# A mixer-and-MLP kernel: first weight matrix in three loads, and another order of loads, products and engines

## The chip, the core and the metric

The kernel runs on one core of one Trainium2 chip. The metric is device time in microseconds (us) of one execution. Five executions of the kernel before took 136.20, 135.62, 136.43, 135.65 and 136.16 us: median 136.16. One further view, the profile, is of one execution that took 136.2 us, of which the program's own instructions span 134.9; the remaining 1.3 us lie around them.

The core has five engines that run side by side and meet at semaphores. TensorE (PE) multiplies matrices; its weight loads are shown as PEld. VectorE (DVE), ScalarE (ACT) and GpSimd (POOL) work elementwise. SyncE (SP) only issues transfers (DMAs). DMAs of one issuing queue are served in the order of their issue.

## What is computed

`x` has 2048 rows (tokens) of 512 bfloat16 numbers. The weights are `w1` and `w2` (512 x 512), `w3` (512 x 1792) and `w4` (1792 x 512).

```python
def reference(x, w1, w2, w3, w4):
    B, S, D = x.shape
    h = _gelu(_layernorm(x, axis=-1) @ w1)
    c = D // 4
    g0 = jnp.pad(h[:, :, 0*c:1*c], ((0, 0), (1, 0), (0, 0)))[:, :S, :]
    ...
    g3 = jnp.pad(h[:, :, 3*c:   ], ((0, 0), (0, 2), (0, 0)))[:, 2:, :]
    hs = jnp.concatenate([g0, g1, g2, g3], axis=-1) @ w2
    x1 = x + hs
    h2 = _gelu(_layernorm(x1, axis=-1) @ w3) @ w4
    return x1 + h2
```

The four quarters of `h` are shifted by 1, -1, 2 and -2 tokens before they meet `w2`. So the second product of a tile of tokens needs `h` of that tile and of both its neighbours.

## The kernel before, in words

**Tiles.** The tokens are cut into 16 tiles of 128, called t0 to t15. A tile passes these steps; q is the tile's number in the first layer and 16 plus the number in the second.

1. Load `dma_x` (line 366), and statistics by `ln` (line 380). For q in `STAT_ACT` ScalarE makes the sums (lines 389 and 394) and DVE two small instructions; for the others DVE does it with `bn_stats` and `bn_aggr` (lines 410 and 412). POOL raises the variance to -1/2 (line 417).
2. Normalization on the engine that `NORM` names: DVE (line 438, the default), ACT (line 447) or POOL (line 450). For the last two, DVE or POOL (`NMR`) first makes one more small number (line 443). Tile 0 is special (`NAT`, `SPLIT`): its mean alone is subtracted, in two halves of 256 columns (line 428), and the scale is applied later, in the gelu (line 562).
3. Transposition. q = 0 to 5, 16 and 17 are transposed on PE with an identity matrix (steps `sa`, `sb` and `ty`, line 483), and copied out of PSUM by DVE or ACT (line 491, choice `EVAC`). The other 24 are transposed by a DMA, `tp`q (line 456), issued by SP after the normalization.
4. `up1`: the product with `w1` (line 619; for tile 0 steps `ra` and `rb`, line 521, each over two of the four K chunks of 128), gelu on ACT (line 634). Tile 0's result is turned by step `th` (line 587).
5. `mix`: the product with the shifted `h` and `w2` (line 659), and the residual on DVE (lines 666 and 670).
6. The same normalization and transposition for the second layer, then `up2` (line 619, 56 matmuls for one group) and gelu.
7. `down` (line 688, 14 matmuls a tile), residual on DVE (line 696), and the store (line 699). The last tile's product is done in pieces of 256, 128 and 128 columns.

`GROUPS` says how many tiles `up1` and `up2` take at once: a group of one streams 128 columns a matmul, of two 256, of four 512.

**What sets the order.** `SCRIPT` is the order of PE's work, written out; PE follows it strictly. It begins with `warm`, products of zeros that need no data. `LOADS` is the order of the input loads, all on SP's queue but `x0`, which ACT issues. An entry `tp`n in `LOADS` stands for that DMA transpose where there is one: tp9 for example is tied between its neighbours, while `tp16` names a tile that PE turns and has no effect. The order on the other engines comes from a planner (`Program.order` and `Program.place`), which runs when the program is built. It walks through a model of the engines with a cost for each operation (`dur`), and at each step gives an engine the ready operation with the smallest due time; due times are counted back from PE's script, starting at `DUE`. Loads get numbers far below all due times (line 736), so SP issues a load whenever one is free to go, and DMA transposes after that. An entry tied ahead of a load inherits a number below that load's (lines 141 to 143). `RESTART` adds time in the model to a load that follows something else than a load on its queue. What the planner leaves is a fixed order for each engine.

`emit` (line 766) writes that order with semaphore waits. A weight load is complete only when all its pieces are; `up2` waits for all four K chunks of `w3`, `down` for all fourteen of `w4`.

Of the kernel before, what the change touches and what calls it, by code (L numbers as in the profile page):

```python
# [25 lines left out]
class Program:  # L26
# [2 lines left out]

    HOP = {"pe": 200.0, "dve": 155.0, "act": 220.0, "pool": 120.0, "sp": 70.0}  # L30
    LOOK = {"dve": 300.0, "act": 300.0}
    DUE = 385824.0
    BEGIN = {"sp": 30.0, "act": 150.0, "pe": 400.0, "dve": 150.0, "pool": 450.0}
    ENTRY = 1900.0
    COLD, RESTART = 4300.0, 800.0
# [16 lines left out]
    def order(self):  # L52
# [58 lines left out]
        assert seen == len(self.ops), "cycle"  # L111
        if self.DUE:

            topo, left = [], [len(d) for d in preds]
            stack = [i for i, n in enumerate(left) if n == 0]
            while stack:
                i = stack.pop()
                topo.append(i)
                for j in succs[i]:
                    left[j] -= 1  # L120
                    if left[j] == 0:
                        stack.append(j)
            due, t = {}, self.DUE
            for op in self.ops:
# [12 lines left out]
        for op in self.ops:  # L137
            op.prio += BIAS.get(op.name, 0.0)
            if op.first is not None:
# [11 lines left out]
    def place(self, succs, order_only):  # L151
# [8 lines left out]
        rings = {"sp": [], "act": []}  # L160
        fed = {}
        clock = moved = last = self.total = 0.0
# [35 lines left out]
        def land(op):  # L198
            nonlocal moved, last
            if op.queue == "tp":  # L200
                at = max(clock + 500.0, op.start + 2450.0, last + 600.0) + self.LAG["tp"]
            elif op.name.startswith("out"):
                at = clock + 300.0
                self.total = max(self.total, at)
            else:
                moved += op.dur
                at = clock + 600.0 + min(600.0, 0.3 * moved) + (600.0 if op.dur > 1400.0 else 0.0) + self.LAG["load"]
            if op.queue != "tp":
                last = max(last, at)
            op.landed = at  # L210
            for j in succs[op.idx]:
                if (op.idx, j) not in order_only:
                    release(op, self.ops[j], at + 30.0)

        while len(out) < len(self.ops):
            while True:
                best = None
                for e in ENGINES:
                    if cands[e]:
                        t = max(free[e], min(ready[o.idx] for o in cands[e]))  # L220
                        if best is None or t < best[0]:
# [12 lines left out]
            if op.queue:  # L234
                tp = op.queue == "tp"
                free[e] = start + (1300.0 if tp else 500.0)
                load = op.name.startswith("dma")
                work = 600.0 if tp else op.dur + (self.RESTART if load and not fed.get(e, True) else 0.0)
                fed[e] = load
                rings[e].append([start + (1400.0 if tp else 1000.0), work, op])  # L240
                for j in succs[op.idx]:
                    if (op.idx, j) in order_only:
                        release(op, self.ops[j], None)
            else:
                dur = op.dur
# [9 lines left out]
        self.seq = out  # L255
        return out

GROUPS = {1: (1, 1, 1, 1, 2, 1, 4, 2, 1, 2), 2: (2, 4, 4, 4, 2)}
NORM = {4: "act", 6: "pool", 8: "pool", 9: "pool", 10: "pool", 12: "act", 14: "pool", 15: "pool", 19: "pool", 20: "pool", 22: "act", 23: "act", 24: "act", 25: "act", 27: "pool", 28: "act", 31: "act"}
EVAC = {1: "both", 2: "dve", 3: "both", 4: "both", 5: "dve", 6: "dve", 8: "both", 11: "dve", 16: "both", 17: "dve", 18: "dve", 20: "dve", 21: "both", 22: "dve", 29: "dve", 30: "dve", 31: "dve"}  # L260
STAT_ACT = (0, 4, 8, 11, 15, 17, 18, 19, 20, 21, 25, 26, 27, 28, 29, 30, 31)
TAIL = (256, 128, 128)
NMR = {1: "pool", 3: "pool", 5: "pool", 10: "pool", 11: "pool", 12: "pool", 13: "pool", 15: "pool", 17: "pool", 20: "pool", 21: "pool", 25: "pool", 26: "pool", 27: "pool", 28: "pool", 30: "pool", 31: "pool"}
NAT = (0,)
SPLIT = (0,)
CSPLIT = ()
HEV = {0: "dve", 2: "dve"}
BIAS = {}
LOADS = """
x1 x2 tp16 w1a w1b x4 x3 w2 x5 x6-7 x9-10 x0@act tp17 x11 w3a w3b x8 w4b w4a tp9 x12-13 x14-15  # L270
"""
SCRIPT = """
warm:10 sa:0 sb:0 ty:1 ra:0 rb:0 ty:2 up1:1 th:0 up1:2 mix:0 ty:3 mix:1 ty:4-5 up1:3-4 mix:2 ty:16-17 mix:3
up2:0 mix:4 up1:5 down:0-1 mix:5 up1:6-7 mix:7-8 up1:9 mix:9-10 up1:8 mix:6 mix:15 up2:1 mix:11-12 up2:2
mix:14 down:4 down:2 down:6 mix:13 up2:4 down:3 down:8 down:5 up2:3 down:7 down:12 down:11 down:10 down:9
down:14 down:13 down:15
"""

def bass_standalone__mixer_s_mlp__prompt_kernel(nc, x, w1, w2, w3, w4, out):
# [14 lines left out]
    with ExitStack() as es:  # L294
        sb = lambda name, shape, dt: es.enter_context(nc.sbuf_tensor(name, shape, dt))
# [22 lines left out]
        warm = sb("warm", [P, 1], F32)  # L318
# [41 lines left out]
        def load(item):  # L360
            name, _, eng = item.partition("@")
            eng = eng or "sp"
            if name[0] == "x":
                a, _, b = name[1:].partition("-")
                t0, t1 = int(a), int(b or a) + 1
                yield pg.add(eng, f"dma_x{t0}", lambda e: e.dma_start(x_sb[:, t0:t1, :], xt[:, t0:t1, :]),
                             writes=[(("x", t), 0) for t in range(t0, t1)], dur=(t1 - t0) * 380.0, queue=eng)
            else:
                dst, src = {"w1": (w1_sb, w1), "w2": (w2_sb, w2), "w3": (w3_sb, w3), "w4": (w4_sb, w4)}[name[:2]]
                n = src.shape[0] // P  # L370
                c0, c1 = {"": (0, n), "a": (0, n // 2), "b": (n // 2, n)}[name[2:]]
                op = pg.add(eng, f"dma_{name}",
                             lambda e: e.dma_start(dst[:, c0:c1, :],
                                                   src.rearrange("(c p) f -> p c f", p=P)[:, c0:c1, :]),
                             writes=[((name[:2], c), 0) for c in range(c0, c1)],
                             dur=(c1 - c0) * P * src.shape[1] * 2 / (345.0 if src.shape[1] == D else 400.0), queue=eng)
                yield op


        def ln(layer, t):  # L380
# [3 lines left out]
            col = lambda a: a[:, q : q + 1]  # L384
            if q in STAT_ACT:
                if layer == 1:
# [22 lines left out]
            else:  # L409
# [4 lines left out]
                       writes=[(("mv", q), 0), (("vpe", q), 0)], dur=75)  # L414
            var = vpe[:, q : q + 1] if q in STAT_ACT else mv[:, q, 1:2]
            pg.add("pool", f"rstd{q}",
                   lambda e: e.tensor_tensor(col(rstd), var, neghalf[:], ALU.pow),  # L417
                   reads=[(("vpe", q), 0), (("neghalf",), 0)], writes=[(("rstd", q), 0)], dur=470)
            how = NORM.get(q, "dve")
            dst = xn_buf[:, slot(q), :]  # L420
# [19 lines left out]
            else:  # L440
                eng = NMR.get(q, "dve")
                pg.add(eng, f"nmr{q}",
# [200 lines left out]
        def mm_mix(t):  # L643
# [220 lines left out]
```

## Time and profile before

| | |
|---|---|
| median of five runs | 136.16 us |
| the profiled execution | 136.2 us |
| its span | 134.9 us |
| PE busy | 131.4 us (97%) |
| ACT, DVE, POOL busy | 61.0, 50.2, 27.5 us |
| read from HBM, written | 6.82 MB, 2.10 MB |
| DMA transposes | 24, median 2.5 us from issue to landing |
| matmuls recorded | 777 |

Times in the profile are us from the span's start, unless marked ns. The page cuts the span into 40 slices of 3.37 us, with a digit for the busy tenths of each engine. A matmul's recorded length includes its passage through the array, so the time that one costs is read from where the next one starts: in the chain of work, sixteen of 128 columns take 0.89 us (0.056 each), 56 of 256 take 6.11 (0.109 each) and eight of 512 take 1.73 (0.216 each). A few matmul records are missing; the chain then shows 0.05 us of "issue" that is no idle time.

### The profile page before, as it was taken

What the parts mean: (1) busy time and instruction counts of PE and PEld (TensorE: products, weight loads), DVE (VectorE), ACT (ScalarE), POOL (GpSimd) and SP (SyncE); (2) the same over time, 40 slices, a digit from 0 to 9 for tenths busy, and PEclk for the clock granted to TensorE, in tenths of its full rate; (3) what the DMA queues carried; (4) which work ended last, traced back from release to release, by engine and by line L of the source; (5) the groups of instructions that cost most, each with busy time, mean ns of one, the idle gap of its engine ahead of it and who ended that gap; (6) DMA issues with size and microseconds to landing.
All of it is one profiled execution on the core that took longest, in us unless ns stands there. A gap on an engine that the chain in (4) does not pass through costs nothing.

```text
span 134.9 us, 2033 instructions
## 1 busy us (share of the span) xinstructions
PE 131.4 (97%) x777; PEld 72.0 (53%) x790; DVE 50.2 (37%) x156; ACT 61.0 (45%) x100; POOL 27.5 (20%) x61
## 2 busy tenths in 40 slices
PE   8999999999999999999999999999999999999994
PEld 3477688544665444444444448844444444444463
DVE  3679988876177810060004226013200002232222
ACT  6678877662527997577554005510055530000000
POOL 2431569499204321006001001000000000000000
PEclk9999999999999999999999999999999999999999
DMA  5899999954551253000300311101110001111112
GB/s 159 266 345 415 363 335 85 222 119 88 110 119 36 45 115 78 0 0 0 78 0 5 78 39 39 39 0 44 39 39 0 0 0 39 39 42 41 39 41 78
DMA packets 21338, 12.20 MB, mean 90 GB/s; under 512 B 13904, under 2 KB 20816, under 8 KB 21328
## 3 DMA queue, kind: packets, MB, share of 16 engines
q1 hardware_dynamic: 20752, 11.80, 34.6%
q10 hardware_dynamic: 576, 0.26, 0.7%
q8 instruction: 6, 0.10, 0.3%
q14 instruction: 4, 0.03, 0.1%
HBM read 6.82 MB, written 2.10 MB: 66 GB/s over the span
## 4 chain that ended last, share of the span: by engine, by line
PE 97%; issue 1%; DVE 0%; POOLq 0%
PE y_ps L619 46%; PE o_ps L688 36%; PE o_ps L659 10%; PE o_ps L712 3%; PE y_ps L483 2%; PE y_ps L521 1%; DVE o_sb L696 0%; PE o_ps L587 0%; POOLq L849 0%
## 5 line engine op out<-in xcount | busy, mean ns | idle before, releaser
L619 PE MATMUL y_ps<-xnT,w_sb 128*128 128x512 bf16 (+2 forms) x420 | 63.4, 308 | 0.2
L619 PEld LDWEIGHTS y_ps<-xnT,w_sb 128*128 128x128 bf16 x424 | 38.3, 98 | 24.9 <-ACT h2T L634 0.3
L688 PE MATMUL o_ps<-w_sb,h2T 128*128 128x512 bf16 (+2 forms) x249 | 48.7, 355 | 0.2
L634 ACT ACTIVATE h2T<-y_ps 128x1024 bf16<-128x1024 f32 (+1 forms) x29 | 28.6, 993 | 24.1 <-PE y_ps L619 23.8
L688 PEld LDWEIGHTS o_ps<-w_sb,h2T 128*128 128x128 bf16 x252 | 23.5, 98 | 24.7
L696 DVE TENSOR_TENSOR o_sb<-o_ps,x_sb 128x512 bf16<-128x512 f32 (+2 forms) x18 | 11.4, 633 | 47.5 <-PE o_ps L688 47.5
L394 ACT ACTIVATE junk<-x_sb 128x512 bf16<-128x512 bf16 x17 | 10.6, 621 | 14.5 <-DVE x_sb L666 14.4
L417 POOL TENSOR_TENSOR rstd<-vpe,neghalf 128x1 f32<-128x1 f32 x17 | 9.4, 559 | 34.5 <-DVE vpe L406 34.5
L666 DVE SCALAR_TENSOR_TENSOR x_sb<-o_ps,x_sb 128x512 bf16<-128x512 f32 x12 | 8.2, 682 | 19.9 <-PE o_ps L659 19.8
L659 PE MATMUL o_ps<-w_sb,hT 128*128 128x512 bf16 x58 | 14.8, 379 | 0.5 <-DVE xn_buf L438 0.3
L417 POOL TENSOR_TENSOR rstd<-mv,neghalf 128x1 f32<-128x1 f32 x15 | 8.2, 548 | 19.5 <-DVE mv L412 18.6
L410 DVE BATCH_NORM_STATS2 st<-x_sb 128x6 f32<-128x512 bf16 x15 | 10.1, 681 | 3.2 <-DMA x_sb<-in_x_dram 3.0
L634 ACT ACTIVATE hT<-y_ps 128x512 bf16<-128x512 f32 (+1 forms) x10 | 8.1, 807 | 6.3 <-PE y_ps L619 6.3
L659 PEld LDWEIGHTS o_ps<-w_sb,hT 128*128 128x128 bf16 x64 | 6.1, 98 | 6.0 <-DVE xn_buf L438 0.2
L438 DVE TENSOR_SCALAR xn_buf<-x_sb,mv,rstd 128x512 bf16<-128x512 bf16 x14 | 6.2, 443 | 4.4 <-POOL rstd L417 4.3
L450 POOL TENSOR_SCALAR xn_buf<-x_sb,rstd,nmr 128x512 bf16<-128x512 bf16 x9 | 7.2, 801 | 1.3 <-DVE nmr L443 0.9
L447 ACT ACTIVATE xn_buf<-x_sb,nmr,rstd 128x512 bf16<-128x512 bf16 x8 | 6.3, 806 | 0.9 <-DVE nmr L443 0.6
L712 PE MATMUL o_ps<-zeros 128*128 128x512 bf16 x10 | 4.4, 632 | 0.6 <-POOLq L849 0.6
L406 DVE SCALAR_TENSOR_TENSOR vpe<-sums,mv 128x1 f32<-128x1 f32 x17 | 2.9, 173 | 3.2 <-ACT junk L394 2.8
L670 DVE TENSOR_TENSOR x_sb<-o_ps,x_sb 128x512 bf16<-128x512 f32 x4 | 2.7, 681 | 3.2 <-PE o_ps L659 3.2
L483 PEld LDWEIGHTS y_ps<-ident,xn_buf 128*128 128x128 bf16 x32 | 2.5, 111 | 1.9 <-issue 0.6
L389 ACT ACTIVATE junk<-x_sb 128x512 bf16<-128x512 bf16 x5 | 3.1, 628 | 1.0 <-DMA x_sb<-in_x_dram 0.8
(34 smaller groups left out, 32.9 us busy)
## 6 DMA issues: line engine op xcount, KB each, us to landing
w_sb<-in_w_dram SPq DMA_DIRECT2D x4, 896.0 KB, 10.9
out_dram<-o_sb SPq DMA_DIRECT2D x15, 128.0 KB, 1.7
x_sb<-in_x_dram SPq DMA_DIRECT2D x4, 256.0 KB, 5.0
x_sb<-in_x_dram SPq DMA_DIRECT2D x7, 128.0 KB, 4.5
w_sb<-in_w_dram SPq DMA_DIRECT2D x2, 256.0 KB, 4.2
w_sb<-in_w_dram SPq DMA_DIRECT2D x1, 512.0 KB, 6.2
xnT<-xn_buf SPq DMA_TRANSPOSE x24, 2.5
x_sb<-in_x_dram ACTq DMA_DIRECT2D x1, 128.0 KB, 2.5
```

The costliest lines, as they stand in the source:

```text
L394: (lambda d: (lambda e: e.activation(d, src, ACT_F.Square, accum_out=sums[:, q, 1:2])))(junk[:, b, :]),
L410: pg.add("dve", f"bnst{q}", lambda e: e.bn_stats(st9[:, q, 0:6], src), reads=rs, writes=[(("st", q), 0)], dur=605)
L417: lambda e: e.tensor_tensor(col(rstd), var, neghalf[:], ALU.pow),
L447: f = lambda e: e.activation(dst, src, ACT_F.Identity, bias=nmr[:, q : q + 1], scale=rstd[:, q : q + 1])
L450: f = lambda e: e.tensor_scalar(dst, src, rstd[:, q : q + 1], nmr[:, q : q + 1], ALU.mult, ALU.add)
L619: ins = e.matmul(y_ps[:, p, W * i : W * (i + 1)], wsb[:, dc, P * fc : P * (fc + 1)], src[:, dc, P * t0 : P * t0 + W], start=(dc == 0), sto ...
L634: (lambda d, s: (lambda e: e.activation(d, s, ACT_F.Gelu_apprx_tanh)))(dst, ysrc),
L659: ins = e.matmul(dst, hT[:, j, c0 : c0 + P], w2_sb[:, j, :], start=(j == 0), stop=(j == DC - 1))
L666: f = lambda e: e.scalar_tensor_tensor(x1_sb[:, t, :], dst, 1.0, x_sb[:, t, :], ALU.mult, ALU.add, accum_out=sums[:, NT + t, 0:1])
L688: ins = e.matmul(dst, h2T[:, fc, P * t : P * (t + 1)], w4_sb[:, fc, cs], start=(fc == 0), stop=(fc == FC - 1))
L696: (lambda d, c: (lambda e: e.tensor_tensor(o_sb[:, oi, c], d, x1_sb[:, t, c], ALU.add)))(dst, cs),
L712: ins = e.matmul(o_ps[:, b, :], zeros[:, 0:P], zeros[:], start=True, stop=True)
```

## The change

`w1` came in two halves (chunks 0-1 and 2-3). Now it comes as a half (`w1a`) and two quarters (`w1r`, `w1s`), with `x0` between them in the list. `w2` and `w3` are cut in the same way, and `w4` into four pieces (3, 4, 3 and 4 of its 14 chunks). `x4-5`, `x13-14` share a load, others come alone.

PE's script has eleven warm-up products instead of ten. The transposes of tile 1 stand between the two halves of tile 0's. t4 and t5 are groups of their own in `up1` where they had been a pair; t6-7 is now a pair, t8-9 a pair, t10-13 four. `mix:4` moves ahead of `up2:0`. In the second layer the groups become (2, 2, 4, 4, 4). The choices of engines are new throughout; the lists are in the diff. The planner charges `RESTART` only where its queue has run dry.

```diff
-    DUE = 385824.0
+    DUE = 316421.0
...
-                work = 600.0 if tp else op.dur + (self.RESTART if load and not fed.get(e, True) else 0.0)
+                dry = load and not fed.get(e, True) and clock + sum(h[1] for h in rings[e]) < start + 800.0
+                work = 600.0 if tp else op.dur + (self.RESTART if dry else 0.0)
...
-GROUPS = {1: (1, 1, 1, 1, 2, 1, 4, 2, 1, 2), 2: (2, 4, 4, 4, 2)}
-NORM = {4: "act", 6: "pool", 8: "pool", 9: "pool", 10: "pool", 12: "act", 14: "pool", 15: "pool", 19: "pool", 20: "pool", 22: "act", 23: "act", 24: "act", 25: "act", 27: "pool", 28: "act", 31: "act"}
-EVAC = {1: "both", 2: "dve", 3: "both", 4: "both", 5: "dve", 6: "dve", 8: "both", 11: "dve", 16: "both", 17: "dve", 18: "dve", 20: "dve", 21: "both", 22: "dve", 29: "dve", 30: "dve", 31: "dve"}
-STAT_ACT = (0, 4, 8, 11, 15, 17, 18, 19, 20, 21, 25, 26, 27, 28, 29, 30, 31)
+GROUPS = {1: (1, 1, 1, 1, 1, 1, 2, 2, 4, 2), 2: (2, 2, 4, 4, 4)}
+NORM = {0: "pool", 8: "act", 10: "act", 12: "pool", 13: "pool", 14: "pool", 15: "pool", 19: "act", 20: "act", 21: "pool", 22: "pool", 25: "act", 26: "act", 29: "act", 30: "act", 31: "pool"}
+EVAC = {0: "dve", 1: "both", 2: "both", 3: "both", 4: "both", 5: "both", 7: "both", 8: "dve", 9: "both", 10: "both", 11: "dve", 12: "dve", 13: "both", 14: "dve", 16: "both", 17: "dve", 18: "dve", 20: "dve", 22: "dve", 23: "dve", 26: "dve", 27: "both", 29: "dve", 30: "both"}
+STAT_ACT = (0, 6, 11, 14, 19, 20, 23, 25, 27, 31)
 TAIL = (256, 128, 128)
...
-HEV = {0: "dve", 2: "dve"}
-BIAS = {}
+HEV = {0: "dve", 4: "dve", 5: "dve"}
+BIAS = {"vpe0": -962.172}
 LOADS = """
-x1 x2 tp16 w1a w1b x4 x3 w2 x5 x6-7 x9-10 x0@act tp17 x11 w3a w3b x8 w4b w4a tp9 x12-13 x14-15
+tp4 x1 x2 w1a tp5 w1r x0@act w1s x3 x4-5 w2a w2r w2s tp3 tp2 tp4 w3a w3r tp5 w4q x9 tp1 x8 x7 x10 x6 w3s x11
+tp1 w4p w4s tp3 x12 w4r tp9 x13-14 x15
 """
 SCRIPT = """
-warm:10 sa:0 sb:0 ty:1 ra:0 rb:0 ty:2 up1:1 th:0 up1:2 mix:0 ty:3 mix:1 ty:4-5 up1:3-4 mix:2 ty:16-17 mix:3
-up2:0 mix:4 up1:5 down:0-1 mix:5 up1:6-7 mix:7-8 up1:9 mix:9-10 up1:8 mix:6 mix:15 up2:1 mix:11-12 up2:2
-mix:14 down:4 down:2 down:6 mix:13 up2:4 down:3 down:8 down:5 up2:3 down:7 down:12 down:11 down:10 down:9
-down:14 down:13 down:15
+warm:11 sa:0 ty:1 sb:0 ra:0 rb:0 ty:2 up1:1 th:0 up1:2 ty:3 mix:0-1 ty:4 up1:3 ty:5 up1:4 mix:2 up1:5 mix:3
+ty:16-17 mix:4 up2:0 up1:6 down:0-1 mix:6 up1:7 mix:5 up1:8 mix:8 mix:7 up2:1 mix:10 mix:9 up1:9 mix:11-12
+up2:2 mix:13 mix:15 up2:3 mix:14 down:5 down:2 down:6 down:3-4 down:7-8 up2:4 down:9 down:12 down:10 down:13
+down:11 down:14-15
 """
...
-                c0, c1 = {"": (0, n), "a": (0, n // 2), "b": (n // 2, n)}[name[2:]]
+                cut = lambda k: k * n // 4
+                a, b = {"": (0, 4), "a": (0, 2), "b": (2, 4), "p": (0, 1), "q": (1, 2), "r": (2, 3), "s": (3, 4)}[name[2:]]
+                c0, c1 = cut(a), cut(b)
```

More of the change, by code (lines that the diff above doesn't have):

```diff
@@ L256, in place @@
         return out
-GROUPS = {1: (1, 1, 1, 1, 2, 1, 4, 2, 1, 2), 2: (2, 4, 4, 4, 2)}
-NORM = {4: "act", 6: "pool", 8: "pool", 9: "pool", 10: "pool", 12: "act", 14: "pool", 15: "pool", 19: "pool", 20: "pool", 22: "act", 23: "act", 24: "act", 25: "act", 27: "pool", 28: "act", 31: "act"}
-EVAC = {1: "both", 2: "dve", 3: "both", 4: "both", 5: "dve", 6: "dve", 8: "both", 11: "dve", 16: "both", 17: "dve", 18: "dve", 20: "dve", 21: "both", 22: "dve", 29: "dve", 30: "dve", 31: "dve"}
-STAT_ACT = (0, 4, 8, 11, 15, 17, 18, 19, 20, 21, 25, 26, 27, 28, 29, 30, 31)
+GROUPS = {1: (1, 1, 1, 1, 1, 1, 2, 2, 4, 2), 2: (2, 2, 4, 4, 4)}
+NORM = {0: "pool", 8: "act", 10: "act", 12: "pool", 13: "pool", 14: "pool", 15: "pool", 19: "act", 20: "act", 21: "pool", 22: "pool", 25: "act", 26: "act", 29: "act", 30: "act", 31: "pool"}
+EVAC = {0: "dve", 1: "both", 2: "both", 3: "both", 4: "both", 5: "both", 7: "both", 8: "dve", 9: "both", 10: "both", 11: "dve", 12: "dve", 13: "both", 14: "dve", 16: "both", 17: "dve", 18: "dve", 20: "dve", 22: "dve", 23: "dve", 26: "dve", 27: "both", 29: "dve", 30: "both"}
+STAT_ACT = (0, 6, 11, 14, 19, 20, 23, 25, 27, 31)
 TAIL = (256, 128, 128)
-NMR = {1: "pool", 3: "pool", 5: "pool", 10: "pool", 11: "pool", 12: "pool", 13: "pool", 15: "pool", 17: "pool", 20: "pool", 21: "pool", 25: "pool", 26: "pool", 27: "pool", 28: "pool", 30: "pool", 31: "pool"}
+NMR = {1: "pool", 2: "pool", 3: "pool", 4: "pool", 5: "pool", 6: "pool", 8: "pool", 12: "pool", 14: "pool", 17: "pool", 18: "pool", 19: "pool", 21: "pool", 26: "pool", 27: "pool", 28: "pool", 29: "pool", 31: "pool"}
 NAT = (0,)
```

## The prediction

> **What bounds the kernel now.** I read the busy shares and slices first, then the chain of work that ended last in order of time, then the transfers one by one with their issue and landing, then the sums by stage.
>
> ```profile
> PE 131.4 (97%) x777; PEld 72.0 (53%) x790; DVE 50.2 (37%) x156; ACT 61.0 (45%) x100; POOL 27.5 (20%) x61
> ...
> PE   8999999999999999999999999999999999999994
> ...
> DVE  3679988876177810060004226013200002232222
> ...
> DMA  5899999954551253000300311101110001111112
> ```
>
> PE is busy 97% of the span, and from the second slice on it has almost nothing to win by being fed better. DVE and the transfers are full only in the first seven slices, some 23 us. So a gain or a loss is made there.
>
> ```profile
> 0.64 4.45 PE o_ps L712 x10
> 5.09 0.85 PE y_ps L483 x8
> 5.94 1.01 PE y_ps L521 x4
> ...
> 9.19 0.27 issue
> 9.46 0.81 PE o_ps L659 x3
> ...
> 11.35 0.31 PE y_ps L483 x4
> 11.66 0.02 issue
> 11.68 0.40 PE y_ps L483 x4
> ...
> 15.58 0.54 PE y_ps L483 x8
> 16.12 0.86 PE o_ps L659 x4
> 16.98 6.11 PE y_ps L619 x56
> 23.10 0.05 issue
> ```
>
> Columns: start, length, what. Three things are to be seen. The ten warm-up products end at 5.09; they start 0.427 us apart, and the eight transposes behind them take 0.106 each where later ones take 0.055, so PE's clock is still the slow one. Between 9.02 and 9.46 PE waits for `w2` (it landed at 9.15: issued at 2.98, 6.18 to landing; the chain puts the wait at 0.27, and one matmul record is missing, so 0.22 is lost). The transposes at 11.35 take 0.73 for eight and those at 15.58 take 0.54, against 0.45: together 0.37 lost, waiting for normalized tiles 4, 5 and 16. Then `up2:0` (16.98) and no wait to the end; the 0.05 at 23.10 is a lost record. All of PE's idle time after the warm-up is thus about 0.6 us, and that bounds what a better order can win.
>
> The loads come next. First the issues on SP's queue (start, length, operation), then, from the listing of DMA issues by stretches of time, the landing of single ones (size, us from issue to landing):
>
> ```profile
> 7.77 4.16 SPq L373 DMA_DIRECT2D w_sb<-in_w_dram  x2
> 17.62 3.58 SPq L456 DMA_TRANSPOSE xnT<-xn_buf  x2
> 21.25 1.09 SPq L366 DMA_DIRECT2D x_sb<-in_x_dram  x2
> 22.79 8.16 SPq L456 DMA_TRANSPOSE xnT<-xn_buf  x6
> ```
>
> ```profile
> w_sb<-in_w_dram SPq DMA_DIRECT2D x1, 896.0 KB, 14.1
> ...
> xnT<-xn_buf SPq DMA_TRANSPOSE x1, 6.1
> ...
> xnT<-xn_buf SPq DMA_TRANSPOSE x1, 4.2
> ...
> xnT<-xn_buf SPq DMA_TRANSPOSE x1, 4.7
> ```
>
> `w4a` is issued at 8.35, lands 14.07 later, at 22.42. The DMA transposes of tile 6 (issued 17.62) and 9 (20.02) stand behind it on the queue: 6.07 and 4.17 to landing, where the median is 2.5, so 23.69 and 24.19. `x12-13` and `x14-15` (21.25, 21.87) land at 24.96 and 25.68, and the third transpose (22.79) only at 27.51. PE reaches tile 6 (`up1:5`) at 23.80 and starts it at 23.83: already before, the data came with nothing to spare.
>
> ```profile
> 10.00:20.00 10.00, 9.93 (x95) 7.52 (x94) 9.34 (x33) 8.18 (x19) 4.33 (x7) 1.00 1.06 374
> 20.00:30.00 10.00, 9.95 (x73) 6.30 (x72) 8.25 (x30) 6.50 (x13) 7.65 (x15) 1.00 1.12 144
> ```
>
> Here (PE, PEld, DVE, ACT, POOL busy with counts, then the granted clock, DMA share, GB/s) DVE is busy 9.34 of 10 us.
>
> **The change part by part.** The columns streamed for data are the same: both cuts of `up1` have six groups of one tile, three of two, one of four; both of `up2` two of two and three of four; transposes and tail are alike. Reordered work is worth nothing in itself: only waits count.
>
> 1. *Start.* One warm-up product more, 0.427 us at the slow spacing, moves the first transpose from 4.88 to 5.31. The slow clock lasts to about 5.98 (two matmuls of `ra` start at 5.87 and 6.14, 0.27 apart instead of 0.216), so two of `sa`, four of `ty:1` at 0.107 run to 5.95, `sb` to about 6.07. Before, `ra` came 0.985 after `sa` (ACT's copy 0.38); now DVE's copy (0.29) gives about 6.2 for `ra`, and `rb` waits some 0.1 for the second copy: end 7.15 against 6.79, **+0.36**. Tile 0's halves move from DVE (0.276 each) to POOL; POOL's row is 0.77 for 512 columns, so about 0.5 each, and with rstd (0.55) ahead, which is ready at 3.48, they are done at 4.0, 4.5, 5.0: hidden by the warm-up. Without that cover, had the halves gone first, tile 1's norm would be late by about 0.1 more. DVE's time saved there (0.55) goes into two more copies. Bounds 0 (the clock rises earlier) and +0.6.
> 2. *`w1` in three.* Both quarters are read by the same step `rb`, which waits for both: no product starts earlier. They are complete with the same 896 KB as before (x0, x1, x2, w1: 5.77), a DMA more; needed at 6.6. Zero; SP issues eight loads more, about 0.47 each, 3.8 us of issuing. The cover is the backlog: issue to landing is 4 to 14 us where an empty queue takes 2.5.
> 3. *`w2`.* Ahead of its end lie the same 1792 KB (x0 to x5, w1, w2) that had landed at 9.53; PE gets to `mix:0` at 7.15 + 2.23 (as before from 6.79 to 9.02) + 0.22 for `ty:3`, 9.61. About 0.09 of wait remains instead of 0.22: **-0.13**, between -0.22 and +0.3 (the transfers before and after it moved 210 to 360 KB a us).
> 4. *Tiles 4, 5, 16.* Two `mix` now precede `ty:4`, `mix:4` comes after `ty:16-17`, and x3 lands earlier than 6.95. All 0.37 goes: **-0.34**, up to +0.3 the other way, because statistics of tile 4 and 17 and the norms of 4 and 6 go from ACT and POOL to DVE (0.68 + 0.19 and 0.41 each), in the stretch with 9.34 of 10.
> 5. *`w3`.* `up2:0` is reached at 16.82 - 0.11 (terms 1, 3, 4) + 0.86 (`mix:4`) + 0.04 (five single tiles instead of three and a pair) = 17.61. `w3s` now stands behind 512 KB of `w4` and lands with 4736 KB. Before, 4352 KB were in at 16.34 and the next 896 KB (`w4b`) at 19.84, so 384 KB more take 1.50: 17.84, and PE starts 0.09 after a landing, as with `w2`. **+0.3**; 0 by the faster rate of `w4a` (2.58 for 896 KB) for the `w4` part, +0.8 if the slowest DMA engines lag more. Here `mix:4`, which covered, is used up.
> 6. *Tiles 6 and 7.* They are now one pair, `up1:6`, wanted straight after `up2:0`: 17.93 + 6.10 = 24.03. Their x comes late in the list (about 16.8 for x6), but their norms, by about 20, are not what decides: both transposes stand behind `w4r`, which ends 6272 KB against 6144: 22.42 + about 0.45 = 22.87. With the distances of before (1.27 to the first, 0.49 to the second) the second lands at 24.63, PE goes on at 24.7: **+0.67**. Bounds 0 and +1.4.
> 7. *The rest.* From there on PE was never waiting; tiles 8 and 9 are wanted at about 32.7, t10-13 at 35.5, `w4` at 26.4, each with 3 us or more after the landing reckoned. The last step is the same. Engine choices there move work among engines that idle (DVE 37%, ACT 45%, POOL 20%). `DUE` shifts all due times alike, `BIAS` moves one instruction of 0.17, the planner's rule costs nothing by itself. 0, between -0.1 and +0.4.
>
> Sum: 0.36 - 0.13 - 0.34 + 0.3 + 0.67 = +0.86. The profiled execution took 136.2 (134.9 and 1.3 around it), the median is 136.16: 137.0.
>
> A rule speaks on term 1. The rows say that the slow clock lasted 5.3 us from the first product at 0.64. The Trainium skill (TensorE: Matmul & The Clock Gate, Part 1: The HAM clock gate) has a busy window of about 3.4 us that runs freely, so that the point of change differs from run to run. With a change at 4.05, 3.4 us after the first product, the eleventh would cost 0.216, and the sum would be 136.8 by this estimate; I keep the row.
>
> **Rivals.**
> - *Loads hidden, no loss* (not slower). The place is term 6, with 5: if `w4r` lands 0.7 us sooner than reckoned and `w3s` 0.4, both waits are gone and -0.11 remains: 136.1. For it: in the fast stretch 896 KB took 2.3 us, and the last 2 us before `w4a`'s landing moved little, which is a straggling DMA engine's lag. Against it: tile 6 was just in time behind 128 KB less. It decides from a second landing before 23.9.
> - *Tile 9 first.* SP takes tp9 as soon as x9 is normalized, and x13-14 and x15, tied behind it, ahead of all other transposes. x9 is four loads ahead of x6. If tp9 goes before tp6, these 384 KB do too: before, the third transpose came 3.3 us after the second, through 512 KB; less 0.4, tile 6 lands at 27.5, a wait of 3.5, sum +3.7: 139.9. For it: the order tp9, x12-13, x14-15, then others, was there before. Against: tile 6 is due far earlier than tile 9, and DVE is too full to take x9 at once.
> - *DVE the bound.* If what DVE takes over isn't hidden, term 4 turns to +0.3 and tiles 6, 7 come later: 137.8. For it the 9.34; against it, 0.9 us more time ahead of `ty:16`.
>
> **How the numbers follow.** Forecast 0.45, hidden 0.23, tile 9 first 0.22, DVE 0.10. The likeliest case alone is 136.4 to 137.6. The range is 135.8 (the hidden case, with half of the 0.6 that terms 1, 3 and 7 may still give at their lower ends) to 139.2, which leaves out most of the 139.9 case and 3 in 100 below.  Half a per cent, what can be told here, is 135.48 to 136.84. Slower: 0.22 + 0.10 + about 0.29 of the forecast's 0.45 = 0.61; faster 0.05, out of the hidden case; the same 0.34.
>
> **What would show it.** `ra` at 6.2 and `up1:1` at about 7.4; no wait at `ty:4`, `ty:5`, `ty:16`; a wait of 0.3 ahead of `up2:0` ended by `w3s`; one of 0.7 ahead of the pair at 24, with the second transpose landing after 24.4; then a dense chain. If the pair starts without waiting, term 6 is wrong; if it starts after 26, tp9 was first; a wait on DVE before 17 means term 4.

## The result, and the profile after

Over all executions on record of the two kernels, the changed kernel's median is 136.76 us (136.30 to 138.26, 28 executions) against 136.11 (135.46 to 136.88, 49). It is slower, by 0.65 us in the medians and 0.89 in the means (136.94 and 136.05), since its times have a longer upper tail. The ratio of the means is 1.0065, with a 95% interval of 1.0049 to 1.0082. The forecast was 137.0, with 0.61 on slower. One execution of all that follow, of 140.77 us in the run that moves `w3s` alone, lay over 1.5% above that kernel's fastest, and is left out of its figures.

The profiled execution of the changed kernel took 136.31 us, with a span of 134.8. That is one of its fastest (136.30 is the lowest of all), while the 136.2 of the profile before lies in the middle of the times of that kernel. So the two profiles, 0.1 us apart, don't show the 0.65 that the medians do. The profile after shows what each step does when the loads come early. That limits everything read from it.

Busy shares and slices of the changed kernel, from the page:

```profile
PE 131.2 (97%) x779; PEld 71.6 (53%) x791; DVE 52.3 (39%) x144; ACT 55.4 (41%) x84; POOL 27.4 (20%) x61
...
PE   8899999999999999999999999999999999999994
...
DVE  3698999785727078100700042232220000232222
...
DMA  6999999954553300520003001211111000111112
```

PE is busy 131.2 us, as before (131.4), and its row of slices differs from before in one digit: the second slice (3.37 to 6.74 us) is 8 where it was 9. What the start loses lies there. The transfers are as full as before, in the same first eight slices.

The chain of work that ended last, in order of time (start, length, what):

```profile
0.09 2.48 DMA x_sb<-in_x_dram
2.59 0.70 DVE st L414
4.14 1.84 POOL xn_buf L432 x2
...
17.75 7.97 PE y_ps L623 x72
```

The chain now begins with the load of x1, its statistics on DVE and then POOL: tile 0's two halves, 1.84 us of them. It goes over to PE at the end of tile 0's products, and from then on it is PE's. `up2:0` starts without a wait: the chain counts it from 17.75, where the matmul before it leaves the array, and its first matmul is recorded at 17.59. This second way of counting is used for all kernels below. The chain takes its 56 matmuls and the 16 of `up1:6` as one piece of 72; a short wait lies between them all the same, as is shown below. The stretch of 10 to 20 us, and SP's queue (issues of the last load but two, `w4r`; of the transposes of tiles 7, 6 and 9; of `x13-14` and `x15`):

```profile
10.00:20.00 10.00, 9.95 (x105) 7.50 (x106) 9.37 (x29) 6.18 (x17) 3.60 (x7) 1.00 1.07 366
```

```profile
13.69 0.44 SPq L377 DMA_DIRECT2D w_sb<-in_w_dram  x1
18.82 3.90 SPq L460 DMA_TRANSPOSE xnT<-xn_buf  x3
22.76 1.09 SPq L368 DMA_DIRECT2D x_sb<-in_x_dram  x2
```

(The columns of the first line are PE, PEld, DVE, ACT, POOL busy with counts, granted clock, DMA share, GB/s.) DVE is 9.37 of 10 us busy (9.34 before). `w4r`, issued at 13.69, landed at 21.93; the transposes landed at 23.23 (tile 7), 23.72 (tile 6) and 24.15 (tile 9). PE wanted the pair 6, 7 at 23.70: the last matmul of `up2:0` starts at 23.59, and such matmuls start 0.109 apart. The first of the pair starts at 23.81, 0.09 behind tile 6's transpose. So PE waited 0.11 for it, its only wait in this profile after tile 0's products.

### The profile page after: what moved, and what is told of

The parts are those of the page before. It is cut to its first block, busy times and chain, and to the rows that moved or that the text cites. A ratio compares the mean times of both kernels' runs of the same rounds, so it can differ in the third digit from the quotient of the medians.

```text
span 134.8 us, 2017 instructions
## 1 busy us (share of the span) xinstructions
PE 131.2 (97%) x779; PEld 71.6 (53%) x791; DVE 52.3 (39%) x144; ACT 55.4 (41%) x84; POOL 27.4 (20%) x61
## 4 chain that ended last, share of the span: by engine, by line
PE 94%; DMA 2%; POOL 1%; issue 1%; DVE 1%; SPq 0%
PE y_ps L623 46%; PE o_ps L692 36%; PE o_ps L663 10%; DMA x_sb<-in_x_dram 2%; POOL xn_buf L432 1%; PE y_ps L487 1%; PE y_ps L525 1%; DVE st L414 1%; DVE o_sb L700 0%; PE o_ps L591 0%; DVE mv L416 0%; POOL rstd L421 0%; SPq L853 0%
## 5 line engine op out<-in xcount | busy, mean ns | idle before, releaser
L421 POOL TENSOR_TENSOR rstd<-mv,neghalf 128x1 f32<-128x1 f32 x22 | 12.1, 553 | 33.6 <-DVE mv L416 32.0
L674 DVE TENSOR_TENSOR x_sb<-o_ps,x_sb 128x512 bf16<-128x512 f32 x10 | 6.9, 685 | 27.0 <-PE o_ps L663 27.0
L414 DVE BATCH_NORM_STATS2 st<-x_sb 128x6 f32<-128x512 bf16 x22 | 14.8, 680 | 2.2 <-DMA x_sb<-in_x_dram 2.0
L421 POOL TENSOR_TENSOR rstd<-vpe,neghalf 128x1 f32<-128x1 f32 x10 | 5.5, 551 | 18.0 <-DVE vpe L410 17.9
L398 ACT ACTIVATE junk<-x_sb 128x512 bf16<-128x512 bf16 x10 | 6.3, 625 | 5.3 <-DVE x_sb L670 5.3
L454 POOL TENSOR_SCALAR xn_buf<-x_sb,rstd,nmr 128x512 bf16<-128x512 bf16 x7 | 5.4, 764 | 1.0 <-DVE nmr L447 0.9
L670 DVE SCALAR_TENSOR_TENSOR x_sb<-o_ps,x_sb 128x512 bf16<-128x512 f32 x6 | 4.1, 682 | 1.3 <-PE o_ps L663 1.3
L416 DVE BATCH_NORM_AGGREGATE mv<-st 128x2 f32<-128x9 f32 x22 | 4.0, 189 | 0.2
L495 ACT ACTIVATE xnT<-y_ps 128x256 bf16<-128x256 bf16 x6 | 2.3, 380 | 2.7 <-PE y_ps L487 2.7
L487 PE MATMUL y_ps<-ident,xn_buf 128*128 128x128 bf16 x32 | 2.9, 220 | 0.4 <-POOL xn_buf L432 0.4
```

The lines of the kernel that those rows point to most:

```text
L398: (lambda d: (lambda e: e.activation(d, src, ACT_F.Square, accum_out=sums[:, q, 1:2])))(junk[:, b, :]),
L414: pg.add("dve", f"bnst{q}", lambda e: e.bn_stats(st9[:, q, 0:6], src), reads=rs, writes=[(("st", q), 0)], dur=605)
L454: f = lambda e: e.tensor_scalar(dst, src, rstd[:, q : q + 1], nmr[:, q : q + 1], ALU.mult, ALU.add)
L674: f = lambda e: e.tensor_tensor(x1_sb[:, t, :], dst, x_sb[:, t, :], ALU.add)
```

## The experiments

In those that change an order, `put(a, b)` takes an operation out of the finished order of its engine and puts it right behind another; a third word names a new engine. "After" is the changed kernel. Each result is the median, with the range and the number of executions in brackets, and then the ratio on record to the kernel before on the same chip, with its 95% interval.

### POOL's two halves: the start

In the profile, tile 0's halves take POOL about twice what I had reckoned, and PE waits for the second. Lines of the changed kernel: the source line of the halves (minimum, median and maximum in ns), POOL's later rows of 512 columns from the page, and PE's instructions around it (start, length, idle before and what ended it).

```profile
L432 POOL TENSOR_SCALAR xn_buf<-x_sb,mv x2: 922/926/929, 4.1 to 5.0; 128x256 bf16<-128x256 bf16 x2
```

```profile
L454 POOL TENSOR_SCALAR xn_buf<-x_sb,rstd,nmr 128x512 bf16<-128x512 bf16 x7 | 5.4, 764 | 1.0 <-DVE nmr L447 0.9
```

```profile
5.12 0.51 PE L487 MATMUL y_ps<-ident,xn_buf 128*128 128x128 bf16 x6
6.02 0.28 PE L487 MATMUL y_ps<-ident,xn_buf 128*128 128x128 bf16 x2 [0.39 <-POOL xn_buf L432]
6.14 1.23 PE L525 MATMUL y_ps<-w_sb,xnT 128*128 128x512 bf16 x4
```

Half a row takes 0.93 us, a whole row later 0.764. So the halves end at 5.07 and 5.97, and PE stands idle for 0.39 ahead of the transposition of the second half.

**The halves back on DVE.**

```diff
+        put("norm0_0", "bnst2", "dve")
+        put("norm0_1", "norm0_0", "dve")
```

> The kernel after, with only the two halves of tile 0's norm taken back from POOL to DVE, ahead of tile 1's norm as in the kernel before; every other order is kept. Theory POOL (these halves last 0.93 us each there, 4.14 to 5.97, and hold the first transposes until 5.12 and 6.02): the transposes start by 5.0 to 5.3, tile 0's products end 0.3 to 0.6 us sooner, the median falls from 136.76 to about 136.2 to 136.4 and the fastest run from 136.3 to about 135.8. Theory queue (transposes of tiles 6 and 7 late behind w4r in most executions): the median stays at 136.7 to 136.8, since what is won at the start is waited for at 24 us.

Measured: 137.23 us (136.83 to 137.64, 6); 1.0085 [1.0063, 1.0108]. Tile 0's products end at about 6.60, some 0.6 earlier than in after, and yet it isn't faster. The gain ran into a wait further on. PE's and ACT's instructions of this kernel, as above:

```profile
18.84 7.36 PE L623 MATMUL y_ps<-xnT,w_sb 128*128 128x256 bf16 x66 [1.53 <-DMA w_sb<-in_w_dram]
```

```profile
17.41 0.63 ACT L393 ACTIVATE junk<-x_sb 128x512 bf16<-128x512 bf16 x1 [1.63 <-DMA x_sb<-in_x_dram]
...
18.04 0.36 ACT L495 ACTIVATE xnT<-y_ps 128x256 bf16<-128x256 bf16 x1
```

`w3s` landed at 18.60 and PE, ready at 17.15, started `up2:0` at 18.84. On ACT something showed that I hadn't seen: the copy for q = 16 (tile 0 of the second layer; line 495), which `up2:0` also needs, stands behind the sum over tile 6 (line 393), and that waited 1.63 us for x6.

**The halves on POOL, in the kernel before.**

```diff
+        put("norm0_0", "rstd1", "pool")
+        put("norm0_1", "norm0_0", "pool")
```

> The kernel before, with only the two halves of tile 0's norm moved from DVE to POOL, between the reciprocal roots of tiles 1 and 2 as in the kernel after. Theory POOL: the halves last 0.9 each, the products of tile 0 start at 6.1 or later, and the median grows by 0.3 to 0.7 us, to 136.4 to 136.8 (ratio 1.002 to 1.005), the fastest run most of all. Theory queue: not over 136.3.

Measured: 136.33 us (136.18 to 136.95, 12); 1.0031 [1.0016, 1.0047], +0.36. The halves take 0.926 here too; the transpositions start at 4.97 and 5.87 and the second waits 0.50. Tile 0's products end at 7.15, where it was 6.79. So this part of the change has a price of its own in the kernel before.

**The halves on POOL with a second operation**, as the rows of 512 columns have it.

```diff
-  e.tensor_scalar(a, b, mv[:, q, 0:1], None, ALU.subtract)
+  e.tensor_scalar(a, b, 1.0, mv[:, q, 0:1], ALU.mult, ALU.subtract)
```

> The kernel after, with tile 0's halves still on POOL but written as x times 1.0 minus mean (two operations) instead of x minus mean alone. Theory form (POOL's subtract with one scalar is the slow thing, 0.93 for 256 columns, while its other normalizations with two scalars take 0.76 for 512): a half takes 0.4 to 0.5, the median falls to about 136.3. Theory early stretch (POOL is slow there because DVE or the loads get in its way): a half still takes 0.9 and the median stays at 136.7.

Measured: 136.74 us (136.41 to 136.94, 9); 1.0053 [1.0035, 1.0071], no different from after. The instruction, by its source line in this kernel:

```profile
L432 POOL TENSOR_SCALAR xn_buf<-x_sb,mv x2: 1146/1148/1150, 4.0 to 5.2; 128x256 bf16<-128x256 bf16 x2
```

With two operations the half takes 1.148, not the 0.4 that half of the later row would be. That a single operation is the slow form is ruled out. Whether it is the subtraction (the later rows multiply and add) or the early stretch, with DVE at work beside it, stays open: I ran no subtraction later, and no addition early.

The run shows one thing more. In its profile tile 0's products end at 7.56, 0.35 later than in after, and `up2:0` starts at 17.93 without a wait, 0.34 later; that execution took 136.74, after's 136.31. But the medians of the two kernels are the same. So in the median a start that is 0.35 later costs nothing that these runs can tell, as if something further on were as late as that anyway.

### What `up2:0` waits for

**`w3s` directly behind `w3r`**, ahead of `w4q` and the x tiles.

```diff
+        put("dma_w3s", "dma_w3r")
```

> The kernel after, with the last quarter of w3 (w3s) issued directly behind w3r, ahead of w4q and the five tiles x9, x8, x7, x10, x6; nothing else moves. The first runs showed no wait for w3s in the profiled execution of after (it landed at 17.10, wanted at 17.75), but 1.69 us in the one with tile 0's halves on DVE (landed 18.60, wanted at 17.15). Theory w3s (its landing differs from run to run, and the late ones make the median 136.76 and the runs up to 138.3): w3s lands before 15, the runs over 137 disappear, and the median falls to 136.3 to 136.5. Theory start (only POOL's slow halves matter): the median stays at 136.7 to 136.8.

Measured: 137.25 us (136.86 to 138.14, 6); 1.0099 [1.0060, 1.0137]. `w3s` landed at 14.16, 2.9 earlier than in after's profile, and nothing was won: x7 came at 16.76 and x6 at 17.50. ACT's and PE's instructions:

```profile
17.53 0.63 ACT L393 ACTIVATE junk<-x_sb 128x512 bf16<-128x512 bf16 x1 [1.34 <-DMA x_sb<-in_x_dram]
...
18.16 0.36 ACT L495 ACTIVATE xnT<-y_ps 128x256 bf16<-128x256 bf16 x1
```

```profile
18.66 7.58 PE L623 MATMUL y_ps<-xnT,w_sb 128*128 128x256 bf16 x68 [0.94 <-DVE mv L416]
```

`up2:0` started at 18.66, 1.10 late, behind ACT's copy, which ended at 18.52. (The bracket names DVE's `mv`, which the product doesn't read.) So there are at least two gates. **The same with the halves on DVE**:

```diff
+        put("dma_w3s", "dma_w3r")
+        put("norm0_0", "bnst2", "dve")
+        put("norm0_1", "norm0_0", "dve")
```

> Both edits: tile 0's halves on DVE, and w3s directly behind w3r. Theory w3s: the 0.6 us that DVE wins at the start is no longer lost at up2:0; no wait there, median 135.6 to 136.0, under the kernel before (135.97 on this chip) or equal to it. The next thing late would be the transposes of tiles 6 and 7 (PE wants them at about 23.2, they land at 23.2 to 24.3): if they bind, 136.0 to 136.6. Rival (halves on DVE delay other DVE work, whatever w3 does): 137.0 to 137.4, as with the halves on DVE alone.

Measured: 138.08 us (137.28 to 138.66, 6); 1.0136 [1.0094, 1.0179]. x7 landed at 17.23, x6 at 17.95, and `up2:0` waited 1.93, to 19.11.

**ACT's copy ahead of the sum over tile 6.**

```diff
+        put("sum6", "ev16act")
```

> The kernel after, with one change in ACT's order: its copy of half of tile 0's second transpose (wanted by up2:0) goes ahead of the first sum of tile 6, which waits for x6 to land. So far up2:0 had a wait in every run where x6 landed at 16.7 or later (up2:0 1.0 to 1.4 us after that landing), or w3s after 17.6. Theory ACT queue (the copy stuck behind tile 6's statistics is what makes after's median and its slow runs): the median falls from 136.76 to 136.3 to 136.45 and no run is over 137. Theory two gates (w3s is late in the same runs, since it follows x6 on the queue): the median falls by 0.1 to 0.2 only, and runs over 137 remain. Theory start (POOL's halves): 136.7 to 136.8.

Measured: 136.80 us (136.38 to 137.89, 12); 1.0079 [1.0052, 1.0107]. In the profile the copy runs at 16.57 and no longer waits; x6 landed at 16.74, but `w3s` at 17.95, and `up2:0` started at 18.19 after waiting 0.74. PE's instruction:

```profile
18.19 8.02 PE L623 MATMUL y_ps<-xnT,w_sb 128*128 128x256 bf16 x72 [0.57 <-ACT junk L398]
```

(The bracket names ACT's sum, which the product doesn't read; the start lies 0.24 behind `w3s`, as in the run with the halves on DVE, where the bracket names the load.) One gate opened, the other held.

**This and the halves on DVE.**

```diff
+        put("sum6", "ev16act")
+        put("norm0_0", "bnst2", "dve")
+        put("norm0_1", "norm0_0", "dve")
```

> The same, and tile 0's halves on DVE (which alone gave 137.23, with x6 at 17.39 and w3s at 18.60 in the profile). Theory ACT queue: 135.7 to 135.9, under the kernel before. Theory two gates: w3s, wanted at 17.15, still holds up2:0, median 136.4 to 137.2, under the 137.23 by little.

Measured: 137.09 us (136.50 to 137.92, 10); 1.0078 [1.0050, 1.0105]. `w3s` landed at 18.26; `up2:0` waited 1.16, to 18.51. A PE that is earlier at the start also waited 0.37 ahead of `ty:3`, from 8.53, and 0.34 ahead of `mix:0`, whose first matmul isn't recorded.

**All three: start, copy and `w3s`.**

```diff
+        put("sum6", "ev16act")
+        put("dma_w3s", "dma_w3r")
+        put("norm0_0", "bnst2", "dve")
+        put("norm0_1", "norm0_0", "dve")
```

> All three edits: the copy ahead of tile 6's sums, tile 0's halves on DVE, w3s directly behind w3r. up2:0 has no late gate left, and starts at about 17.2. Theory two gates and nothing behind them: 135.6 to 135.9. Forecast's term 6 (the pair of tiles 6 and 7 waits for its transposes): x6 lands at about 17.5 to 18, its transpose is issued after 20.5 and lands at 23.3 to 24.5, wanted at 23.3: a wait of 0 to 1.2 there, median 136.0 to 137.0.

Measured: 137.60 us (136.34 to 137.95, 6); 1.0107 [1.0066, 1.0148]. Both gates were open (`w3s` at 14.46), and `up2:0` still started at 18.35. DVE's instructions of this kernel:

```profile
17.08 0.69 DVE L414 BATCH_NORM_STATS2 st<-x_sb 128x6 f32<-128x512 bf16 x1 [1.03 <-DMA x_sb<-in_x_dram]
17.69 0.60 DVE L495 COPY xnT<-y_ps 128x256 bf16<-128x256 bf16 x2
```

A third gate: the other copies that `up2:0` needs stand on DVE behind the statistics of tile 7, and these waited 1.03 us for x7, which landed at 17.05.

**`w4q` behind `w3s`.** All three gates hang on loads that stand behind `w4q`, 512 KB of `w4` that no product wants before 25 us. Here it goes behind them, with the halves on DVE.

```diff
+        put("dma_w4q", "dma_w3s")
+        put("norm0_0", "bnst2", "dve")
+        put("norm0_1", "norm0_0", "dve")
```

> The kernel with tile 0's halves on DVE (137.23 when that was its only edit), and one load moved: w4q (512 KB of w4, first wanted at 25 us) goes behind w3s instead of ahead of x9, x8, x7, x10, x6 and w3s. So far three different gates held up2:0, each in its turn: w3s itself, ACT's copy behind the sums that wait for x6, DVE's copies behind the statistics that wait for x7. Theory load order (all three are late for one reason, the 512 KB ahead of them): x7, x6 and w3s land 1.3 to 2 us sooner, by 14.5, 15 and 16.5, up2:0 starts at about 17.2 without a wait, and the median falls by 0.7 to 1.3 us from 137.23, to 136.0 to 136.5; what remains is term 6, the pair of tiles 6 and 7, wanted at 23.3, with transposes that land behind w4r at 23.7 to 24.6. If that does not bind either, 135.6 to 135.9. Theory other (more work on DVE at the start is what costs): 137.0 to 137.4.

Measured: 137.34 us (136.59 to 137.79, 10); 1.0086 [1.0055, 1.0116]. PE's instructions of this kernel:

```profile
5.30 1.06 PE L487 MATMUL y_ps<-ident,xn_buf 128*128 128x128 bf16 x8
...
10.46 1.89 PE L663 MATMUL o_ps<-w_sb,hT 128*128 128x512 bf16 x8 [0.55 <-ACT hT L638]
...
18.35 1.91 PE L623 MATMUL y_ps<-xnT,w_sb 128*128 128x256 bf16 x16
```

The gates open as expected: x7 at 14.79, x6 at 15.55, `w3s` at 16.73, and `up2:0` starts without a wait. But it starts at 18.35, since PE had lost the time earlier: `w2s` landed at 10.21, 1.0 later than in after, and `mix:0` waited 0.71. The line names ACT's gelu as the end of that wait, but in after's profile `mix:0` is under way 0.23 after that same gelu began, before its 0.60 were over, so it isn't what the product needs; `w2s` is what was late. And all eight first transpositions run at half the clock (1.06 for eight), so the start's gain isn't there either. A load tells of its landing in 16 shares; 15 of those of `w2s` had come by 9.35, and the last at 10.21. Why that one was late in this run, with the same loads ahead of it as in after, I couldn't show.

### Tiles 6 and 7

**`w4r` behind the transposes of tiles 7, 6 and 9.**

```diff
+        put("dma_w4r", "tp9")
```

> The kernel after, with the last quarter of w4 (w4r, 384 KB) issued by SP behind the transposes of tiles 7, 6 and 9 instead of ahead of them; nothing else moves. Theory queue: the transposes land about 1 us sooner (22.2 and 22.7 instead of 23.2 and 23.7), runs over 137.2 disappear and the median falls by 0.2 to 0.4. Theory POOL: the median stays at 136.7 to 136.8. w4r must still land before 25.8, where down:0 wants it; if it does not, the time grows by what is missing.

Measured: 137.58 us (137.32 to 138.22, 6); 1.0114 [1.0090, 1.0139]. The transposes of tiles 7 and 6 landed at 21.82 and 23.11 instead of 23.23 and 23.72. That won nothing: PE wanted the pair at 24.23 only, since `up2:0` had waited 0.56 for `w3s` (17.87), and `down:0` then waited 1.14 for `w4r`, which landed at 26.65.

In the profiles that keep `w4r` ahead, tile 6's transpose is close to being a gate of its own. PE waited for it where `up2:0` started earliest: 0.11 in after, 0.135 with two operations on POOL and 1.35 in the run with 22 warm-ups below. In six of the other seven it landed only 0.07 to 0.25 us before PE wanted the pair. So opening the gates of `up2:0` alone, with the transposes landing as they did, could have won little more than that.

### The quarters of `w1`

**The kernel before with its second half of `w1` as two quarters**, and nothing else (besides the names of the quarters in the loader).

```diff
-x1 x2 tp16 w1a w1b x4 x3 w2 x5
+x1 x2 tp16 w1a w1r w1s x4 x3 w2 x5
```

> The kernel before, with the second half of w1 as two quarters and nothing else. Forecast and all theories: no difference (ratio 0.998 to 1.002), because the same step of PE waits for both. Rival (a DMA more delays the loads behind it by a transfer's fixed share, 0.3 us or more): w2 lands later than 9.4, and the time grows by 0.2 to 0.4.

Measured: 136.52 us (135.95 to 137.30, 12); 1.0033 [1.0010, 1.0057]. x4 landed at 6.52 (6.11 before), x3 at 7.60 (6.95), `w2` at 9.74 (9.15). DVE's and PE's instructions of this kernel:

```profile
7.62 0.69 DVE L410 BATCH_NORM_STATS2 st<-x_sb 128x6 f32<-128x512 bf16 x1 [1.69 <-DMA x_sb<-in_x_dram]
8.23 0.41 DVE L491 COPY xnT<-y_ps 128x512 bf16<-128x512 bf16 x1
```

```profile
8.70 1.07 PE L619 MATMUL y_ps<-xnT,w_sb 128*128 128x128 bf16 x16 [0.41 <-DVE xnT L491]
9.83 1.02 PE L659 MATMUL o_ps<-w_sb,hT 128*128 128x512 bf16 x4
```

The first two show the same shape as at `up2:0`: the copy that PE wants next (line 491) stands on DVE behind statistics that wait 1.69 us for x3. PE stood 0.57 before `up1:2`. But that isn't what the time hangs on: `up1:2` was done at 9.60, and `mix:0` started at 9.83, 0.09 behind `w2`. That is 0.59 later than in before, with its unrecorded first matmul put at 9.24, and the two executions lie 0.54 apart. So the rival was right in place, and nearly in size. How much of the landing is the cut's doing, one profile of each doesn't tell: with the list of loads unchanged and the halves on POOL, x4 landed at 6.43, x3 at 6.78 and `w2` at 8.72.

### The warm-up as more, smaller products

This one has 22 warm-up products of 256 columns instead of 11 of 512, so that PE has issued eleven products and eleven weight loads more by the same time (not 22 of each, as the expectation has it). It was to show whether the fetch of PE's instructions, which uses the same DMA engines, is what delays some landings.

```diff
-                for _ in range(n):
-                    ins = e.matmul(o_ps[:, b, :], zeros[:, 0:P], zeros[:], start=True, stop=True)
+                for _ in range(2 * n):
+                    ins = e.matmul(o_ps[:, b, 0:256], zeros[:, 0:P], zeros[:, 0:256], start=True, stop=True)
```

> The kernel after, with 22 warm-up products of 256 columns instead of 11 of 512: the same PE time, 22 matmuls and 22 weight loads more in PE's stream of instructions. Theory fetch (in every trace one 16 KB instruction packet takes 1.1 us of one DMA engine when PE has issued some 270 to 300 instructions, at 14.7 to 16.5 us; where that comes ahead of w3s on that engine, w3s lands about 1.2 us later): the packet starts earlier, at about 14 to 15.5, w3s lands at 18 or later, median 137.2 to 137.8. Rival (the fetch is tied to something else, or w3s's spread has another source): median 136.6 to 136.9.

Measured: 138.29 us (137.81 to 139.19, 6); 1.0158 [1.0121, 1.0195], the slowest of all. A 16 KB packet of instructions came at 15.15 instead of 16.53 and a second one at 22.52 instead of 25.91. But the loss isn't at `up2:0` (0.165 there; `w3s` at 17.57). PE's instructions of this kernel:

```profile
25.27 1.91 PE L623 MATMUL y_ps<-xnT,w_sb 128*128 128x256 bf16 x16 [1.18 <-ACT h2T L638]
```

It is at the pair 6, 7: tile 6's transpose landed at 25.18, 0.09 before the pair starts (the gelu that the bracket names had ended at 24.77), and 1.95 after tile 7's where it is 0.5 in after. The second packet lies in that stretch. That the fetch is what held it up is argued, not shown: all 16 shares of that transpose came within 0.2 us, so no single late DMA engine is to be seen, and the run also changed the start.

## Why the prediction was right, and where it wasn't

Sign and size were right (137.0; 136.76). The sum reached the right size partly with the wrong terms, and so partly by luck.

- **Term 1, the start, +0.36.** Right in size (tile 0's products end at 7.21, forecast 7.15, before 6.79), wrong in cause. I charged an eleventh warm-up product and the slow clock. A product of 512 columns takes 0.427 at the slow clock and 0.216 at the fast one; in this run the tenth, at 4.46, took 0.260, so the clock rose at about 4.55, and the eleventh cost half. What cost the time is POOL's halves at 0.93 where I had taken 0.5 from the row of 512 columns and called them hidden by the warm-up. Moved alone in the kernel before, they cost +0.36. On the clock, the free-running window of about 3.4 us that I had weighed from the Trainium skill (TensorE: Matmul & The Clock Gate, Part 1: The HAM clock gate) was the better guide, in that the point of change differs from run to run. Read in the same way, it lies at 3.38 (halves on DVE, ACT's copy ahead), 3.65 (halves on DVE), 4.55 (after), 5.98 (before) and 6.54 (`w4q` moved), with the first product at 0.63 to 0.64 each time: 2.7 to 5.9 us after it, the earliest before 3.4 us had passed. The row of one run wasn't a property of the kernel.
- **Term 2, the quarters, zero.** Wrong as measured in the kernel before: +0.33% [0.10, 0.57]. The step that failed is "the cover is the backlog": in that profile the loads behind the cut landed later though its issue is hidden, and `mix:0` waited for `w2`. In after's own profile nothing of the kind shows: `w1` in three was complete at 5.71 (5.77 before), and the 1792 KB up to the end of `w2` at 9.19 (9.53 before). What the quarters cost in after's median wasn't tried.
- **Term 3, `w2`, -0.13.** Right; in the profile `mix:0` doesn't wait at all (-0.22: `w2s` at 9.19, wanted at 9.70). In the run with `w4q` moved it waited 0.71, beyond the +0.3 that I had as the other end.
- **Term 4, tiles 4, 5, 16, -0.34.** Right: no wait at any of them.
- **Term 5, `w3`, +0.3.** The right place: PE reaches `up2:0` at 17.59 (forecast 17.61). The landing was well reckoned on the mean: 17.84 forecast; the seven profiled kernels with after's order up to `w3s` have 17.10, 17.19, 17.57, 17.87, 17.95, 18.26 and 18.60, mean 17.79. After's own profile is the earliest of them, and has no wait. In the five that waited for it PE started 0.24 to 0.25 after the landing, not 0.09. What I missed are two further gates at the same product, ACT's copy behind tile 6's sum and DVE's copies behind tile 7's statistics. I had looked at what PE waits for in the transfers and not at what stands ahead of its copies on ACT and DVE.
- **Term 6, tiles 6 and 7, +0.67.** The right mechanism, too large: 0.11 in after, 0.135 in the run with two operations on POOL, 1.35 with 22 warm-ups alone. Tile 6's transpose does follow `w4r`, by 1.79 to 2.13 us in nine of the ten profiles with `w4r` ahead (1.76 forecast). The step that failed is the landing of `w4r`, 22.87 forecast and 21.93 measured, and with it that of the transpose, 24.63 against 23.72. In the six profiles with after's whole order of loads `w4r` landed at 21.84 to 22.86 and that transpose at 23.72 to 25.18: the forecast lay at the late end. And where `up2:0` starts later than the 17.93 of the forecast, the pair is wanted later too: with the halves on DVE a landing at 24.78 cost nothing.
- **Term 7** holds: from the pair on PE is dense.

Of the rivals, "loads hidden" is what the profiled execution comes near. Its span is 0.06 less than before's; terms 1, 3 and 4 and the 0.11 of term 6 give +0.42 - 0.22 - 0.34 + 0.11 = -0.03. The median isn't that run. What I said there for it, that a straggling engine holds up the end of `w4a`, was misread: all 16 shares of `w4a` landed between 22.22 and 22.42. What makes the last 2 us ahead of that slow stays open. "Tile 9 first" fell: SP takes tiles 7, 6, then 9, and `x13-14` behind them. "DVE the bound" fell in its form: DVE isn't too busy, but waits for x7, with copies queued behind.

What stays open is how the 0.65 of the medians divides in the changed kernel. Shown are, each by itself on the kernel before, the POOL halves (1.0031, some 0.42 us; 0.36 in the medians) and the quarters (1.0033, some 0.45); and that `up2:0` can be up to 1.9 us late in kernels close to after. They don't add up: a late start hides in a later wait, as the run with two operations on POOL shows. In the profiles without a long wait behind it, the kernel's time follows the start of `up2:0`: 17.59 and 136.31, 17.93 and 136.74, 18.19 and 136.88, 18.51 and 137.33, 18.66 and 137.20, 18.84 and 137.64, so 118.5 to 118.8 behind it. (The three others lie at 118.8 to 119.0; the two with later waits at 119.6 and 120.0.) By that, after's median would belong to a start at about 18.05, 0.45 later than in its profile. The mean landing of `w3s` and 0.25 give 18.04. So term 5 fits as what makes the median, but that is argued: no profile of a median run of after was taken.

Why kernels with the earlier start aren't faster is shown only in part: in all of them the loads x6 and x7, or `w2s`, came later than in after's run, and tile 6's transpose stood close behind. Whether a busier start makes the loads late, or these runs just drew it, isn't settled. No version tried here beats the kernel before.

## What to carry to other kernels

An engine's fixed order is a queue: when you look for what gates a product, list what stands ahead of its copies on every engine, and whether any of that waits for a load; opening one gate here only showed the next. A load that isn't wanted soon delays all the loads behind it: with the halves on DVE, x6 and `w3s` landed 1.84 and 1.87 us sooner once `w4q` stood behind them. An issue that is hidden doesn't make a split free; it cost 0.33% here. Look also at the gate behind the one that you open. One profile is one draw: see where its time stands among the executions before you take a clock, a landing or a zero from it.

## What the runs showed of the hardware that was not expected

- POOL took 0.926 us to subtract a column from 128x256 (0.922 to 0.930 in two kernels), and 1.148 to multiply and subtract, early on, and 0.764 to multiply and add over 128x512 later.
- With the same list of loads up to it, one load's landing (`w3s`) varied by 1.5 us between the profiles of seven kernels, 17.10 to 18.60. In each, the last of its 16 shares came 0.04 (after) to 1.09 (halves on DVE) behind the one before it.
- With nothing changed but a load cut in two (128 KB each), the time was 0.33% longer [0.10, 0.57]. The tiles behind it landed 0.4 and 0.65 us later, but one profile of each kernel is too little: with the list unchanged these landings differed by 0.3 and 0.2 between two kernels.
- The rise of TensorE's clock came between 2.7 and 5.9 us after the first product.
- Instructions come in packets of 16 KB over the DMA engines of the data, some 1.1 us long on one of them. With the halves on DVE one came at 14.70; x7 landed at 15.62 with its last share 0.13 behind the others, and the last share of x10, the next load, came 1.05 behind them (15.98 and then 17.03). With ACT's copy ahead one came at 16.15, and the last share stayed 0.4 us behind the others, as it was before. That the packet causes such a delay is argued, not shown.
